# Windowed attention into mixture-of-experts attention on one core: gate, softmax-sum and scale arithmetic moved from VectorE to GpSimd, with a new written-out order

## The chip, the cores and the metric

One core of one Trainium2 chip runs the whole program. A core has TensorE (matmuls, PE in the profile, with PEld for its weight loads), VectorE (DVE), ScalarE (ACT), GpSimd (POOL) and SyncE (SP, which here only issues transfers). The metric is the device time of one execution in microseconds; lower is better.

## The reference

Eight batches of 576 positions. First every head does attention in a sliding window of 64 positions; its eight heads side by side are the input of a layer of four attention experts. A gate picks two of the four experts for each position and weights them.

```python
def _attn_ref(q, k, v):                      # 8 batches, 8 heads, 576 positions, 64 columns
    scores = scale * np.matmul(q, k.transpose(0, 1, 3, 2))
    mask = (rel >= 0) & (rel < 64)
    scores = np.where(mask, scores, -1000000000.0)
    attn = np.exp(scores - np.max(scores, axis=-1, keepdims=True))
    attn = attn / (np.sum(attn, axis=-1, keepdims=True) + 1e-09)
    return np.matmul(attn, v)
...
def _moe_ref(x, w_gate, wq, wk, wv, wo):     # x: 8 x 576 x 512, 4 experts of 64 columns
    logits = x @ w_gate
    topk = np.argpartition(-logits, K, axis=-1)[..., :K]
    w = np.exp(sel)                          # sel: the two chosen logits less the greater
    w /= w.sum(-1, keepdims=True) + 1e-09
    for e in range(E):
        a = np.exp(scores - scores.max(-1, keepdims=True))    # causal
        a /= a.sum(-1, keepdims=True) + 1e-09
        ye = a @ v @ wo[e]
        out += mask[..., None] * w[:, :, kk:kk + 1] * ye
```

## The kernel before

The work is cut into named units, each a Python generator whose steps (from one `yield` to the next) issue a few instructions. A written-out string, `ORDER`, names the unit whose next step is recorded next. Each engine runs its own instructions in just that order, in sequence: an instruction that waits holds back all that stand behind it on its engine. A colon in `ORDER` gives the PSUM banks that the unit takes.

Stage 1 (windowed attention) goes in 72 groups `g` of four tiles. `m` makes scores on TensorE; `q` is `s1_qk`: VectorE adds the mask and finds the row minimum (L320) and, from group 18 on, folds two halves (L328); ScalarE takes exponentials and row sums into `st` (L331); VectorE adds 1e-9 to the sums (L339) and takes the reciprocal (L340); GpSimd multiplies the rows by it (L344). `t` transposes on TensorE and VectorE masks while it copies out (L381); `a` multiplies by the values, and VectorE leaves the rest of a split in two (L405).

Stage 2 goes by batch `b` and pair of experts `pr`. `v` projects values, `g` is `s2_gate`, `k` and `r` project keys and queries, `x` makes scores on TensorE (L609), `y` is `s2_soft`: VectorE masks and finds the minimum (L624), ScalarE takes exponentials (L628). `u` is `s2_w`: for the row sums in `r2` VectorE adds 1e-9 (L658), takes the reciprocal (L659) and multiplies by the gate (L660); then for each of nine rows x ScalarE writes the scaled row as float16 (L671, `hi`), and what float16 leaves (`lo`) comes either from GpSimd in two instructions (L676, L677) or from VectorE in one (L674). `LOW` says which for each row, and from batch 6, pair 1 on (`LATE`) it is VectorE for all. `D` are transposing transfers of `hi` and `lo`, issued by SP; `A` multiplies them by the values on TensorE (L708), and `o` makes the output (L494 to L496 with the weights `wo`).

Stage 1 of later batches runs beside stage 2 of earlier ones, so from about 60 us on all engines work on both. Batch 7 has nothing of stage 1 left beside it.

Of the kernel before, what the change touches and what calls it, by code (L numbers as in the profile page):

```python
# [13 lines left out]
OP = mybir.AluOpType  # L14
AX = mybir.AxisListType
# [5 lines left out]
E = 4  # L21
# [9 lines left out]
LOW = "PPPPPPPPP"  # L31
LATE = (6, 1)


UP = 2.0 ** 15
# [130 lines left out]
def window_attention_moe_attention(ctx: ExitStack, tc: tile.TileContext, qT, kT, vW,  # L166
                                   wg, wq, wk, wv, wo, out):
    nc = tc.nc
# [681 lines left out]
```

## Time and profile before

| | |
|---|---|
| runs | median 484.28 us of 3 (483.62 to 485.56) |
| the profiled execution | 485.02 us, of which the profile's span is 483.3 us |
| mean granted TensorE clock in it | 0.973 of full speed |
| busy in the span | PE 444.5 us, DVE 423.9 us, ACT 357.2 us, POOL 323.9 us |

The span runs from the first to the last instruction that the profiler saw; what lies around it is 1.7 us. An engine's busy time is the time in which it worked on at least one instruction. Neighbours can overlap a little, so the durations of a list's lines add up to somewhat more than the busy time.

### The profile page before, as it was taken

Reading aid. Unit: us, or ns where it says so; the run is one execution under the profiler, and the core shown is the slowest. Engines: PE = TensorE matmul, PEld = TensorE weight load, DVE = VectorE, ACT = ScalarE, POOL = GpSimd, SP = SyncE. Lnnn points to the kernel's source line nnn. Section 1 sums busy time; section 2 is a strip of 40 time slices with the busy share of each in tenths; the row PEclk is TensorE's granted clock in tenths of the full one; section 3 lists DMA queues with packets and bytes.
Section 4 is the critical chain, followed back from the end, with each engine's and each line's share of the span. In section 5 each row is a group of like instructions: output and inputs, shape, how many; then the busy total and the mean of one; then the engine's idle time right before and its main releaser. Section 6 shows DMA issues by size and latency. Waiting matters only on the chain.

```text
span 483.3 us, 17081 instructions
## 1 busy us (share of the span) xinstructions
PE 444.5 (92%) x6192; PEld 391.7 (81%) x6192; DVE 423.9 (88%) x1784; ACT 357.2 (74%) x1304; POOL 323.9 (67%) x682
## 2 busy tenths in 40 slices
PE   7999999989999898988989989989999899999846
PEld 6787898978889798777978979878898779888745
DVE  4797999999999999999998999999999897997730
ACT  5987998787985675786786768767796666768722
POOL 4899698987799758776789575795878676400000
PEclk9999999999999899999999999999999899989959
DMA  8883276968996696766879769386697866468893
GB/s 259 321 306 105 92 158 185 154 173 167 229 213 144 111 224 213 146 148 172 165 181 169 171 160 263 107 154 176 149 203 134 151 138 137 73 110 159 171 174 110
DMA packets 142788, 81.86 MB, mean 169 GB/s; under 512 B 124656, under 2 KB 125680, under 8 KB 142704
## 3 DMA queue, kind: packets, MB, share of 16 engines
q1 hardware_dynamic: 142624, 80.64, 73.1%
q8 instruction: 49, 0.80, 0.7%
q14 instruction: 35, 0.29, 0.2%
q10 hardware_dynamic: 80, 0.13, 0.1%
HBM read 40.90 MB, written 9.44 MB: 104 GB/s over the span
## 4 chain that ended last, share of the span: by engine, by line
DVE 56%; PE 21%; POOL 7%; issue 5%; DMA 5%; ACT 4%; SPq 1%; DVEq 0%; POOLq 0%; ACTq 0%
DVE pt L381 12%; DVE p L624 8%; DVE sm L320 6%; PE ps L708 4%; PE ps L609 4%; DVE p L328 4%; DMA k<-in_kT_dram 3%; DVE xl L405 3%; PE ps L494 3%; PE ps L394 2%; PE ps L496 2%; DVE vr L515 2%; PE ps L495 2%; ACT p L628 2%; PE ps L303 2%
## 5 line engine op out<-in xcount | busy, mean ns | idle before, releaser
L677 POOL TENSOR_TENSOR sp<-p,sp 128x192 f16<-128x192 f32 (+3 forms) x104 | 96.8, 931 | 8.7
L628 ACT ACTIVATE p<-p,r 128x192 f32<-128x192 f32 (+3 forms) x128 | 77.2, 607 | 21.9 <-DVE r L624 15.0
L344 POOL TENSOR_SCALAR p<-p,st 128x64 f32<-128x64 f32 x216 | 64.3, 322 | 32.4 <-DVE st L340 17.8
L331 ACT ACTIVATE p<-p,st 128x64 f32<-128x64 f32 x216 | 72.4, 339 | 17.2 <-DVE p L328 13.3
L671 ACT ACTIVATE sp<-p,r 128x192 f16<-128x192 f32 (+3 forms) x128 | 72.3, 609 | 9.2 <-DMA tu<-sp 6.2
L381 DVE TENSOR_TENSOR pt<-ps,tri 64x512 f32<-64x512 f32 (+1 forms) x120 | 75.5, 633 | 2.8 <-PE ps L394 0.8
L676 POOL TENSOR_SCALAR p<-p,r 128x192 f32<-128x192 f32 (+3 forms) x104 | 63.0, 606 | 17.1 <-ACT sp L671 17.1
L708 PE MATMUL ps<-tu,v 128*64 128x64 f16 (+2 forms) x1760 | 64.4, 233 | 8.7 <-DMA tu<-sp 6.7
L624 DVE CUSTOM_DVE_ANT_0 p<-ps,causal 128x320 f32<-128x320 f32 (+3 forms) x160 | 67.8, 470 | 4.3 <-PE ps L609 2.6
L708 PEld LDWEIGHTS <-v 128*64 128x64 bf16 x1760 | 60.8, 114 | 12.5 <-DMA tu<-sp 6.8
L320 DVE CUSTOM_DVE_ANT_0 sm<-ps,win 128x128 f32<-128x128 f32 x264 | 62.3, 282 | 4.0 <-PE ps L303 2.3
L609 PE MATMUL ps<-kt,qt 64*128 64x256 f32 (+2 forms) x480 | 54.3, 333 | 7.8 <-DVE kt L579 2.4
L609 PEld LDWEIGHTS ps<-kt,qt 64*128 64x128 f32 x480 | 37.8, 185 | 18.6 <-issue 2.6
L303 PE MATMUL ps<-k,q 64*64 64x128 f32 (+1 forms) x1080 | 40.9, 280 | 5.2 <-DMA k<-in_kT_dram 2.8
L303 PEld LDWEIGHTS ps<-k,q 64*64 64x64 f32 x1080 | 31.9, 138 | 12.0 <-issue 4.1
L331 ACT ACTIVATION_READ_ACCUMULATOR p<-p,st 128x1 f32 x216 | 41.2, 191 | 0.0
L494 PE MATMUL ps<-xh,wkhi 128*128 128x320 f32 (+1 forms) x128 | 39.7, 310 | 1.5 <-DVE st L320 0.7
L494 PE MATMUL ps<-xh,wqhi 128*128 128x256 f32 (+1 forms) x128 | 39.3, 307 | 1.5 <-DVE yl L717 0.8
L487 POOL MEMSET sp<- 128x256 f16 (+2 forms) x38 | 10.7, 291 | 44.4 <-DMA tu<-sp 32.7
L394 PE MATMUL ps<-pt,v 128*64 128x64 f32 x1080 | 39.1, 227 | 1.4 <-DVE r L624 0.9
L394 PEld LDWEIGHTS ps<-pt,v 128*64 128x64 f32 x1080 | 34.8, 140 | 6.9 <-DVE r L624 1.3
L496 PE MATMUL ps<-xh,wqlo 128*128 128x256 f32 (+1 forms) x128 | 37.8, 296 | 0.0
(140 smaller groups left out, 1265.8 us busy)
## 6 DMA issues: line engine op xcount, KB each, us to landing
v<-in_vW_dram SPq DMA_DIRECT2D x30, 576.0 KB, 4.9
k<-in_kT_dram SPq DMA_DIRECT2D x29, 320.0 KB, 4.2
q<-in_qT_dram SPq DMA_DIRECT2D x29, 288.0 KB, 3.4
out_dram<-out SPq DMA_DIRECT2D x32, 256.0 KB, 2.7
tu<-sp SPq DMA_TRANSPOSE x96, 3.7
out_dram<-out SPq DMA_DIRECT2D x7, 128.0 KB, 2.5
sp<-in_kT_dram SPq DMA_DIRECT2D x2, 320.0 KB, 6.6
p<-in_qT_dram SPq DMA_DIRECT2D x2, 288.0 KB, 6.4
```

The source lines that it names most:

```text
L303: nc.tensor.matmul(S1[g][i][o:o + 64, c:], lhsT=q_t[r, 64 * b:64 * b + 64], rhs=k_t[r, 64 * b + c:64 * b + 128], start=True, stop=True)
L320: nc.vector.tensor_tensor_reduce(out=to, in0=ps[i][:, c:], in1=win[:, int(b == 0), c:], scale=-0.125, scalar=3.0e38, op0=OP.add, op1=OP.mi ...
L331: nc.scalar.activation(pt[:, i], pt[:, i], AF.Exp, bias=st[:, 0, z + i:z + i + 1], scale=-1.0, accum_out=st[:, 1, z + i:z + i + 1])
L381: nc.vector.tensor_mul(t[64 * w:64 * w + 64, :n, e], ps[r, :n], tri[r, w, None, :].to_broadcast([64, n, 128]))
L394: nc.tensor.matmul(o[64 * h:64 * h + 64, 4 * x + i], lhsT=pairs[p][2][:, h, b], rhs=t[:, i, c:c + 64], start=True, stop=True)
L494: nc.tensor.matmul(ps, lhsT=ah, rhs=bh, start=first, stop=False)
L609: nc.tensor.matmul(ps[e][:, at(i):at(i) + n], lhsT=QT[pr][r, w, q], rhs=KT[b, pr][r, m, key:key + n], start=x == 0, stop=x == 2)
L624: nc.vector.tensor_tensor_reduce(out=dst, in0=src, in1=mask, scale=1.0, scalar=3.0e38, op0=OP.add, op1=OP.min, accum_out=to)
L628: nc.scalar.activation(p, p, AF.Exp, bias=r2[:, 0, x:x + 1], scale=-1.0, accum_out=r2[:, 1, x:x + 1])
L671: nc.scalar.activation(hi, p, AF.Copy, scale=by)
L677: nc.gpsimd.tensor_tensor(lo, p, hi, op=OP.subtract)
L708: nc.tensor.matmul(to, lhsT=V2[b % 2][:, c, a, 2 * pr + h], rhs=rhs, start=n == 0, stop=n == len(work_list) - 1, skip_group_check=True)
```

## The change

Four things change. In `s1_qk` the sum of 1e-9 goes from VectorE to GpSimd, with a step of its own before the reciprocal. In `s2_gate` VectorE keeps the comparisons, the reductions and the reciprocal; the mask product and sum, the subtraction of the maximum, the product with the selection, the 1e-9 and scale, the product with the reciprocal, and the copies into `G2` go to GpSimd, in seven further steps; of two VectorE lines the order is exchanged. In `s2_w` the 1e-9 and the product with the gate go to GpSimd, except from `LATE` on. `LOW` gives row 7 (576 wide) to VectorE, where one instruction takes the place of two on GpSimd. And `ORDER` is another string throughout; two lines of each near its end are shown.

```diff
-LOW = "PPPPPPPPP"
+LOW = "PPPPPPPDP"
...
-    'u701 y710 o54 A601 u700 u700 u700 A611 y710 y710 y710 y710 k711:7 k711 o53 o53 o60:2 u700 u700 D7001 D7001 '
-    'x712:34 x712 k711 k711 x711:57 x711 y711 D7010 D7010 D7011 D7011 u701 o60 u701 A611 A611 A601 A601 u701 u701 '
+    'k711 o53 o53 D7000 D7000 D7010 D7010 D7011 D7011 D7001 D7001 o54 o54 x710:45 x710 x712:31 x712 x711:72 x711 '
+    'u701 y710 y710 y710 y711 u701 u701 u701 u701 u701 y710 y710 y711 y711 o62:6 o60:4 o61:5 o60 o61 D7020 D7020 '
...
-        nc.vector.tensor_scalar_add(st[:, 2, :n], st[:, 1, :n], 1e-9)
+        nc.gpsimd.tensor_scalar(st[:, 2, :n], st[:, 1, :n], 1e-9, 1.0, op0=OP.add, op1=OP.mult)
+        yield
         nc.vector.reciprocal(st[:, 2, :n], st[:, 2, :n])
...
-        nc.vector.tensor_mul(g4[:, 1], g4[:, 1], below[:, None].to_broadcast([128, n, E, E]))
-        nc.vector.tensor_add(g4[:, 0], g4[:, 0], g4[:, 1])
+        yield
+        nc.gpsimd.tensor_tensor(g4[:, 1], g4[:, 1], below[:, None].to_broadcast([128, n, E, E]), op=OP.mult)
+        nc.gpsimd.tensor_tensor(g4[:, 0], g4[:, 0], g4[:, 1], op=OP.add)
+        yield
...
         nc.vector.tensor_reduce(gt[:, 0], g4[:, 0], axis=AX.X, op=OP.add)
+        nc.vector.tensor_reduce(gs[:, 0], lg, axis=AX.X, op=OP.max)
         nc.vector.tensor_scalar(gt[:, 0], gt[:, 0], 1.5, None, op0=OP.is_lt)
-        nc.vector.tensor_reduce(gs[:, 0], lg, axis=AX.X, op=OP.max)
-        nc.vector.tensor_sub(gt[:, 1], lg, gs[:, 0, :, None].to_broadcast([128, n, E]))
+        yield
+        nc.gpsimd.tensor_tensor(gt[:, 1], lg, gs[:, 0, :, None].to_broadcast([128, n, E]), op=OP.subtract)
         yield
         nc.scalar.activation(gt[:, 1], gt[:, 1], AF.Exp)
         yield
-        nc.vector.tensor_mul(gt[:, 1], gt[:, 1], gt[:, 0])
+        nc.gpsimd.tensor_tensor(gt[:, 1], gt[:, 1], gt[:, 0], op=OP.mult)
+        yield
         nc.vector.tensor_reduce(gs[:, 1], gt[:, 1], axis=AX.X, op=OP.add)
-        nc.vector.tensor_scalar(gs[:, 1], gs[:, 1], 1e-9, 1.0 / UP, op0=OP.add, op1=OP.mult)
+        yield
+        nc.gpsimd.tensor_scalar(gs[:, 1], gs[:, 1], 1e-9, 1.0 / UP, op0=OP.add, op1=OP.mult)
+        yield
         nc.vector.reciprocal(gs[:, 2], gs[:, 1])
-        nc.vector.tensor_mul(gt[:, 2], gt[:, 1], gs[:, 2, :, None].to_broadcast([128, n, E]))
+        yield
+        nc.gpsimd.tensor_tensor(gt[:, 2], gt[:, 1], gs[:, 2, :, None].to_broadcast([128, n, E]), op=OP.mult)
...
-            nc.vector.tensor_copy(dst[0:64], src[64:128])
-            nc.vector.tensor_copy(dst[64:128, 0:3], src[0:64, 1:4])
+            nc.gpsimd.tensor_copy(dst[0:64], src[64:128])
+            nc.gpsimd.tensor_copy(dst[64:128, 0:3], src[0:64, 1:4])
...
-        nc.vector.tensor_scalar_add(r2[:, 2, x], r2[:, 1, x], 1e-9)
+        engine = nc.vector if (b, pr) >= LATE else nc.gpsimd
+        engine.tensor_scalar(r2[:, 2, x], r2[:, 1, x], 1e-9, 1.0, op0=OP.add, op1=OP.mult)
+        yield
         nc.vector.reciprocal(r2[:, 2, x], r2[:, 2, x])
-        nc.vector.tensor_mul(r2[:, 3, x], r2[:, 2, x], G2[b % 2][:, pr, x])
+        yield
+        engine.tensor_tensor(r2[:, 3, x], r2[:, 2, x], G2[b % 2][:, pr, x], op=OP.mult)
         yield
```

What stands on VectorE at the gate of batch 3 before the change, with row scales of batches 2 and 3 (`r2`) beside it (`gt` and `gs` are the gate's tiles, `g2` its result, `yl` and `xl` rests of splits that TensorE waits for):

```order
L405 TENSOR_TENSOR xl4_4012<-ps_67,xh4_4011 128x512
L542 TENSOR_TENSOR gt_3_0_3957<-gt_3_0_3957 128x16
L543 TENSOR_REDUCE gs_3_0_3958<-gt_3_0_3957 128x4
L544 TENSOR_SCALAR gs_3_0_3958<-gs_3_0_3958 128x4
L545 RECIPROCAL gs_3_0_3958<-gs_3_0_3958 128x4
L546 TENSOR_TENSOR gt_3_0_3957<-gt_3_0_3957,gs_3_0_3958 128x16
L551 COPY g2_1_90<-gt_3_0_3957 64x4x2x2
L552 COPY g2_1_90<-gt_3_0_3957 64x3x2x2
L554 COPY g2_1_90<-gt_3_0_3957 64x2 x2
L717 TENSOR_TENSOR yl1_86<-ps_67,yh1_84 128x320
L658 TENSOR_SCALAR r2_3_0_3872<-r2_3_0_3872 128x7
L659 RECIPROCAL r2_3_0_3872<-r2_3_0_3872 128x7
```

Nine small instructions of the gate stand in a row here, ahead of `yl1`. After the change VectorE has, at the same gate (lines 390 and up are those of the new file; `qt` and `kt` are rests that the scores on TensorE wait for):

```order
L677 RECIPROCAL r2_2_1_3363<-r2_2_1_3363 128x2
L390 TENSOR_TENSOR pt1_44_4107<-ps_67,tri_78 64x2x128
L609 TENSOR_TENSOR qt0_81<-ps_67,qt0_81 128x256
L595 TENSOR_TENSOR kt_3_0_3837<-ps_67,kt_3_0_3837 128x256
L390 TENSOR_TENSOR pt1_43_4112<-ps_67,tri_78 64x4x128
L560 RECIPROCAL gs_3_0_3950<-gs_3_0_3950 128x4
L390 TENSOR_TENSOR pt1_44_4107<-ps_67,tri_78 64x2x128
L390 TENSOR_TENSOR pt1_43_4112<-ps_67,tri_78 64x4x128
```

Only the reciprocals are left, and each stands among large instructions that wait for other things. On GpSimd, at the same place, the order before has only large work of rows (`p2`, `px`) and of stage 1 (`p1`):

```order
L344 TENSOR_SCALAR p1_45_4004<-p1_45_4004,st1_44_3933 128x64 x4
L487 MEMSET sp1_72 128x4x64
L676 TENSOR_SCALAR p2_1_69<-p2_1_69,r2_2_1_3454 128x576
L677 TENSOR_TENSOR sp1_72<-p2_1_69,sp1_72 128x576
L676 TENSOR_SCALAR p2_1_69<-p2_1_69,r2_2_1_3454 128x576
L677 TENSOR_TENSOR sp1_72<-p2_1_69,sp1_72 128x576
L676 TENSOR_SCALAR px_70<-px_70,r2_3_0_3872 128x64
```

After the change the same stretch of GpSimd reads:

```order
L675 TENSOR_SCALAR r2_2_1_3363<-r2_2_1_3363 128x2
L679 TENSOR_TENSOR r2_2_1_3363<-r2_2_1_3363,g2_0_89 128x2
L558 TENSOR_SCALAR gs_3_0_3950<-gs_3_0_3950 128x4
L353 TENSOR_SCALAR p1_45_3826<-p1_45_3826,st1_44_3813 128x64 x4
L695 TENSOR_SCALAR p2_1_69<-p2_1_69,r2_2_1_3363 128x448
L696 TENSOR_TENSOR sp1_72<-p2_1_69,sp1_72 128x448
L562 TENSOR_TENSOR gt_3_0_3949<-gt_3_0_3949,gs_3_0_3950 128x16
L567 COPY g2_1_90<-gt_3_0_3949 64x4x2x2
L568 COPY g2_1_90<-gt_3_0_3949 64x3x2x2
L570 COPY g2_1_90<-gt_3_0_3949 64x2 x2
L675 TENSOR_SCALAR r2_3_0_4042<-r2_3_0_4042 128x7
```

The small instructions now stand here, between the rows' work, and those at L679, L558 and L562 wait for VectorE. The third place is the start of GpSimd's work on stage 1 (`sm` are the first groups' rows, `st` their sums). Before:

```order
L344 TENSOR_SCALAR sm1_0_151<-sm1_0_151,st1_0_150 128x128 x4
L344 TENSOR_SCALAR sm1_1_225<-sm1_1_225,st1_1_224 128x128 x4
L344 TENSOR_SCALAR sm1_2_237<-sm1_2_237,st1_2_236 128x128 x4
L344 TENSOR_SCALAR sm1_3_249<-sm1_3_249,st1_3_248 128x128 x4
L479 MEMSET v2_1_91 64x768
```

And after:

```order
L488 MEMSET v2_0_92 64x768
L347 TENSOR_SCALAR st1_0_179<-st1_0_179 128x4
L353 TENSOR_SCALAR sm1_0_180<-sm1_0_180,st1_0_179 128x128 x4
L347 TENSOR_SCALAR st1_1_185<-st1_1_185 128x4
L353 TENSOR_SCALAR sm1_1_186<-sm1_1_186,st1_1_185 128x128 x4
L347 TENSOR_SCALAR st1_2_205<-st1_2_205 128x4
L347 TENSOR_SCALAR st1_3_209<-st1_3_209 128x4
L353 TENSOR_SCALAR sm1_2_206<-sm1_2_206,st1_2_205 128x128 x4
```

Each group's rows now have an addition ahead of them on GpSimd, with VectorE's reciprocal between the two.

## Rows read from the trace of the kernel before

**Rows 1.** The page's first part: busy time, share of the span and instructions by engine.
```profile
PE 444.5 (92%) x6192; PEld 391.7 (81%) x6192; DVE 423.9 (88%) x1784; ACT 357.2 (74%) x1304; POOL 323.9 (67%) x682
```

**Rows 2.** Windows: length, each engine's busy time (instructions), clock, DMA share, GB/s.
```profile
60.00:400.00 340.00, 319.07 (x4548) 283.26 (x4548) 324.89 (x1321) 258.61 (x970) 263.66 (x535) 0.99 0.78 170
...
20.00:40.00 20.00, 19.53 (x325) 17.13 (x319) 16.48 (x79) 16.45 (x63) 18.52 (x46) 1.00 0.63 221
40.00:60.00 20.00, 19.75 (x286) 17.05 (x287) 18.00 (x102) 18.43 (x71) 15.36 (x40) 1.00 0.35 110
...
400.00:420.00 20.00, 20.00 (x211) 19.03 (x207) 16.31 (x63) 14.58 (x45) 12.28 (x19) 1.00 0.54 94
420.00:440.00 20.00, 18.89 (x259) 16.47 (x259) 17.68 (x75) 13.00 (x39) 0.94 (x3) 0.91 0.65 124
```

**Rows 3.** PE's waits, 60 to 400 us: us in total, times, longest.
```profile
PE ps L494 <- DVE vr L515: 2.5, 3, 1.4
...
PE ps L494 <- ACT yh L715: 1.1, 1, 1.1
...
PE ps L494 <- DVE pt L381: 0.2, 1, 0.2
```

**Rows 4.** The page's fourth part: the chain that ended last, by engine.
```profile
DVE 56%; PE 21%; POOL 7%; issue 5%; DMA 5%; ACT 4%; SPq 1%; DVEq 0%; POOLq 0%; ACTq 0%
```

**Rows 5.** VectorE's groups, 60 to 400 us: count, busy us, mean ns, idle before.
```profile
L660 DVE TENSOR_TENSOR r<-r,g 128x7 f32<-128x7 f32 (+1 forms) x24 | 8.5, 355 | 0.8
L658 DVE TENSOR_SCALAR r<-r 128x7 f32<-128x7 f32 (+1 forms) x24 | 7.3, 303 | 0.2
L339 DVE TENSOR_SCALAR st<-st 128x8 f32<-128x8 f32 x27 | 6.4, 236 | 0.3 <-ACT p L331 0.2
L531 DVE TENSOR_TENSOR g<-g,below 128x64 f32<-128x64 f32 (+1 forms) x9 | 5.7, 635 | 0.3
...
L552 DVE COPY g<-gt 64x12 f32<-64x12 f32 x6 | 1.0, 162 | 0.1
```

**Rows 6.** Timeline, VectorE and GpSimd near 221 us, and VectorE late: start, us.
```profile
221.44 1.29 POOL L677 TENSOR_TENSOR sp<-p,sp 128x576 f16<-128x576 f32 x1
...
221.70 1.05 DVE L660 TENSOR_TENSOR r<-r,g 128x7 f32<-128x7 f32 x1
...
452.36 0.17 DVE L660 TENSOR_TENSOR r<-r,g 128x7 f32<-128x7 f32 x1
```

**Rows 7.** GpSimd's groups by form, 60 to 400 us; last, one of the whole run.
```profile
L344 POOL TENSOR_SCALAR p<-p,st 128x64 f32<-128x64 f32 x216 | 64.3, 322 | 32.4 <-DVE st L340 17.8 <-ACT p L331 4.7 <-PE ps L609 3.0
L677 POOL TENSOR_TENSOR sp<-p,sp 128x576 f16<-128x576 f32 x24 | 31.0, 1291 | 2.0
...
L676 POOL TENSOR_SCALAR p<-p,r 128x576 f32<-128x576 f32 x24 | 19.1, 797 | 11.9 <-ACT sp L671 11.9
...
L677 POOL TENSOR_TENSOR sp<-px,sp 128x64 f16<-128x64 f32 x13 | 4.3, 329 | 1.1
...
L474 POOL MEMSET below<- 128x16 f32 x1 | 0.1, 118 | 0.0
```

**Rows 8.** Groups by form, whole run: one operation on both engines, and VectorE's row rest.
```profile
L519 POOL TENSOR_TENSOR v<-vr,v 128x256 bf16<-128x256 f32 x28 | 19.8, 706 | 2.3
...
L519 DVE TENSOR_TENSOR v<-vr,v 128x256 bf16<-128x256 f32 x4 | 2.8, 688 | 0.1
...
L674 DVE SCALAR_TENSOR_TENSOR sp<-p,r,sp 128x576 f16<-128x576 f32 x6 | 4.7, 812 | 3.5 <-DMA tu<-sp 3.5
```

**Rows 9.** Windows: the first 8 to 52 us, columns as in the second group.
```profile
8.00:52.00 44.00, 41.15 (x629) 34.84 (x629) 35.22 (x197) 37.86 (x160) 38.66 (x94) 0.96 0.67 240
```

**Rows 10.** Timeline of PE near the end: start, us, count, idle before.
```profile
465.19 2.61 PE L708 MATMUL ps<-tu,v 128*64 128x256 f16 x50 [6.68 <-DMA tu<-sp]
```

**Rows 11.** Waits of SP's queue, whole run: us in total, times, longest.
```profile
SPq L685 <- POOL p L676: 30.3, 20, 4.6
SPq L685 <- POOL sp L677: 27.5, 17, 3.0
```

More of the change, by code (lines that the diff above doesn't have):

```diff
@@ L550, in s2_gate @@
             dst = G2[b % 2][:, :, 1:9].rearrange("r p (j s) -> r j p s", s=2)
-            nc.vector.tensor_copy(dst[0:64], src[64:128])
-            nc.vector.tensor_copy(dst[64:128, 0:3], src[0:64, 1:4])
+            nc.gpsimd.tensor_copy(dst[0:64], src[64:128])
+            nc.gpsimd.tensor_copy(dst[64:128, 0:3], src[0:64, 1:4])
             for s in range(2):
-                nc.vector.tensor_copy(G2[b % 2][64 * s:64 * s + 64, :, 0], src[0:64, 0, :, s])
+                nc.gpsimd.tensor_copy(G2[b % 2][64 * s:64 * s + 64, :, 0], src[0:64, 0, :, s])
         else:
             for h in range(2):
-                nc.vector.tensor_copy(G2[h][64:128, :, 7:9], src[64 * h:64 * h + 64, 0])
+                nc.gpsimd.tensor_copy(G2[h][64:128, :, 7:9], src[64 * h:64 * h + 64, 0])
     def proj(b, name, pr, half):
```

251 rows, old and new, of the table ORDER are left out of this document.

## The prediction

> **What bounds the kernel now.** I read the page's busy times first [rows 1]: PE is busy for 92% of the span and DVE for 88%, so neither alone explains the time. The windows show how they share it [rows 2]. Between 60 and 400 us, where stage 1 and stage 2 run side by side, DVE works for 324.9 of 340 us (95.6%) and PE for 319.1. PE's waits in that stretch [rows 3] say why PE is idle for the other 20.9 us: of 21 lines all but one (ACT, 1.1 us) name a DVE instruction that TensorE's next matmul needs or whose PSUM bank it takes over. The chain that ended last goes through DVE for 56% of its length and through PE for 21% [rows 4]. So in the middle DVE is the engine that is out of time and PE follows it. POOL is busy for 263.7 of the 340 us there (78%).
>
> The two ends are different. From 8 to 52 us POOL has the work: 38.7 of 44 us, against 35.2 on DVE [rows 9]. Near the end PE stands still for 6.68 us, waiting for transposing transfers of `hi` and `lo` [rows 10]; POOL has almost nothing left then.
>
> **What the change takes from VectorE.** Thirteen lines of DVE go to POOL. Between 60 and 400 us they are, from L660 (24 times, 8.5 us) down to L552 (6 times, 1.0 us), 159 instructions and 51.9 us [rows 5]. That is 0.33 us for each of these tiny instructions, and the timeline shows what is in it: L660 took 1.05 us at 221.70 and ended within 0.02 us of POOL's 1.29 us instruction that had begun at 221.44; late, with POOL idle, the same instruction took 0.17 us [rows 6]. Some of what leaves DVE is thus time spent standing behind POOL.
>
> What comes to DVE is row 7's rest, 13 instructions, 12 of them in this stretch. Beside an idle POOL one takes 0.81 us [rows 8]. Beside a busy one it reads two tiles as L660 does, so it may stand behind a POOL instruction of up to 1.29 us [rows 7]: bounds 10 and 25 us for the twelve. I take 1.0 us each, 12 us, since L660's mean excess over its undisturbed 0.17 us is 0.19 us. Net, DVE goes from 324.9 to 285 us (bounds 283 and 298).
>
> How much of PE's idle time does that return? I take it from stretches of this run where DVE has less work than PE. In 20 to 40, 40 to 60, 400 to 420 and 420 to 440 us DVE has 0.84, 0.91, 0.82 and 0.94 of PE's busy time, and PE is idle for 0.47, 0.25, 0.00 and 1.11 us: 1.8 of 80 us, 2.3% [rows 2]. The middle would go from 1.02 to 285/319 = 0.89, so I give it that 2.3%: 7.8 us idle in place of 20.9, **a gain of 13 us**. Bounds: 19 (PE idle 2 us, nothing but a last remainder) and 0.
>
> **What the change gives to GpSimd.** There is no POOL row for additions or copies this small. From above: no instruction of 64 columns takes more than 0.33 us; from below: a memset of 16 columns takes 0.12 us [rows 7]. Between them I draw lines through two widths: L344 at 64 and L676 at 576 columns (0.322 and 0.797 us) give 0.26 us plus 0.9 ns a column, L677 (0.329 and 1.291 us) gives 0.21 us plus 1.9 ns. At 2 to 64 columns that is 0.21 to 0.33; I take 0.25 us on average. 159 of them cost 40 us. Row 7 takes away 12 times 0.797 and 12 times 1.291 us, 25 us. POOL goes from 263.7 to 279 us, 82% of the stretch. From below it is 257 us; from above, with the 0.08 us that stands idle ahead of each L677 (2.0 us in 24) added to each new one, 304 us, 89%. POOL was 93% busy between 20 and 40 us (18.5 of 20) and PE lost 0.47 us, so 82% alone costs nothing. I put **0** here; the hand-offs are a rival below.
>
> The Trainium skill says otherwise: GPSIMD Engine Reference, section 4.1 (Engine selection), puts elementwise work of two inputs on VectorE, GpSimd being about twice as slow. One operation stands on both engines here, L519, and took 706 ns on POOL and 688 ns on DVE [rows 8]; that row doesn't show the factor. By this page of the Trainium skill the 51.9 us would become 104 us on POOL, which would need 239 + 104 = 343 us for the 340.
>
> **The new waits.** A softmax sum now goes ACT, POOL, DVE, POOL instead of ACT, DVE, POOL; a row's scale goes POOL, DVE, POOL; a gate crosses between DVE and POOL seven times. Behind DVE's waiting reciprocals stand the rests `kt` and `qt` that the scores wait for; behind POOL's L558 and L562 stand the rows that SP's transfers wait for. The order places other work between, and PE waits only if a whole engine runs late.
>
> **The start.** By 52 us POOL also has 18 additions for the first groups and 11 instructions of batch 0's gate, 29 at 0.25 us: 7.3 us. It is idle for 5.3 of the 44 us [rows 9], so between 2 and 7 us of this come on top if PE has nothing else. I take **3 us lost**, near the lower bound, because the order also moves a clearing of `v2` into POOL's first idle time.
>
> **The end.** From `LATE` on nothing moves. After the scores `x711` the old order leaves PE `x713`, three outputs and the two products `A70`, the new one four outputs and the same; the transfers for `A710` hang on the same DVE and ACT work. **0**, bounds 2 gained and 4 lost.
>
> **Sum.** The profiled execution took 485.0 us. 485.0 - 13 + 3 = 475.0 us; the median lies 0.7 us below that execution, so **474.3 us**. This case's own range is 467 to 481: below, 19 gained in the middle and 2 lost at the start; above, 7 lost at the start and, in the middle, 3 of the 11 us that the slice at 0.94 (5.5% idle, 18.9 us) would add to 7.8.
>
> **Rivals.**
>
> *GpSimd becomes the bound (slower).* POOL takes each of its instructions in turn, and each new one may wait for DVE. DVE was the bound at 95.6% of the stretch; POOL reaches that share of 340 us when a new instruction costs (325 - 239)/159 = 0.54 us with its wait, and from there all of the gain is gone. At 0.55 us the middle takes 341 us, and the start's 29 cost 16 us against 5.3 idle, 11 us lost: 485.0 + 1 + 11 - 0.7 = 496 us. For it: every new instruction depends on another engine's. Against it: the prices above, and POOL's 78% now. The factor of two in the Trainium skill (GPSIMD Engine Reference, section 4.1) leads to the same place, 343 us for POOL. Chance 0.16.
>
> *The waits move, the time stays.* PE stops waiting for DVE and waits for what POOL feeds. SP's transfers already wait 27.5 and 30.3 us for POOL's row instructions [rows 11], and a net 15 us of POOL work in front of them makes these later. If PE's idle time stays near 20 us, the gain of 13 becomes 0 and the start's 3 us are made up by the order: 484 us. Against it: L708, which uses these transfers, waited for one only once, at the end [rows 10]. Chance 0.12.
>
> *TensorE alone is the bound.* In 400 to 420 us PE lost nothing at a ratio of 0.82 [rows 2]. If the middle loses 2 us in all, and POOL's start hides behind other work: 485.0 - 19 - 0.7 = 465 us. Chance 0.11.
>
> *The forecast.* Chance 0.61.
>
> **How the numbers follow.** A measurement of this kernel tells a change from none at about 0.5%, 2.4 us. Faster holds the forecast and TensorE's case, 0.72; the case without gain is 0.12; slower is 0.16. The range runs from 465, TensorE's case, less one, to 488: this holds the forecast's own 467 to 481 and the case without gain; what it leaves out is most of the GpSimd rival and a little below 464, less than 2 in 10.
>
> **What would show it.** Right: DVE busy near 385 us in all and under 90% of the middle; PE's waits on DVE there 8 us or less; POOL between 330 and 355 us, with L347 and L675 at 0.23 to 0.27 us; the thirteen new L693 near 1.0 us. Wrong in the middle: PE's idle time there still above 15 us, or named by POOL. Wrong at the start: PE idle more than 5 us between 20 and 60 us. What would make the prediction wrong altogether is a POOL instruction of few columns that takes 0.5 us or more, copies between partition halves above all, for which nothing in this trace has a price.

## The result, and the profile after

The changed kernel took 467.68 us (median of 4 runs, 466.91 to 468.84) beside 483.95 us for the kernel before on the same chip: a ratio of 0.9661 (95% interval 0.9629 to 0.9692). The profiled execution took 467.63 us, 17.4 us less than that of the kernel before.

The page's busy times, to lay beside [rows 1], and the chain by engine, beside [rows 4]:

```profile
PE 438.8 (94%) x6192; PEld 388.9 (83%) x6192; DVE 376.6 (81%) x1588; ACT 357.2 (77%) x1304; POOL 347.3 (75%) x865
...
PE 21%; DVE 9%; ACT 8%; POOL 7%; DMA 4%; issue 3%; SPq 0%; DVEq 0%; POOLq 0%; ACTq 0%
```

DVE works 47.3 us less than before, POOL 23.4 us more. The chain's shares add up to 52% here, since it could be followed back no further than 218 us; before they add up to 99%. So 9% is not to be held against the 56% of [rows 4] as it stands: of the part that was followed, DVE has 9 of 52, an estimated 17%. Windows of the changed kernel, columns as in [rows 2]:

```profile
0.00:60.00 60.00, 54.10 (x719) 46.09 (x720) 39.38 (x221) 45.90 (x189) 49.37 (x145) 1.00 0.57 196
60.00:385.00 325.00, 313.40 (x4584) 279.94 (x4584) 288.58 (x1186) 260.74 (x976) 279.76 (x676) 1.00 0.79 179
385.00:465.90 80.90, 71.30 (x896) 62.88 (x894) 48.59 (x182) 50.57 (x140) 18.20 (x46) 0.94 0.75 146
```

And the two stretches of the kernel before that stand around its 60 to 400 us in [rows 2]:

```profile
0.00:60.00 60.00, 55.08 (x808) 46.82 (x809) 45.85 (x267) 49.24 (x198) 46.06 (x124) 0.97 0.63 216
400.00:483.30 83.30, 70.32 (x846) 61.60 (x842) 53.18 (x198) 49.38 (x137) 14.15 (x25) 0.91 0.67 133
```

Subtract PE's busy time from each length. At the start PE was idle for 4.9 us and now is for 5.9; in the middle 20.9 and now 11.6; at the end 13.0 and now 9.6. Together this is 11.7 us less idle time. (How it divides is rough, since the stretches of the two kernels hold nearly, not quite, the same work.) The other 5.7 us are in PE's busy time, 444.5 against 438.8 for the same 6192 matmuls. In the middle DVE is now at 88.8%, and POOL at 86%.

PE's waits of the changed kernel, 60 to 385 us (beside [rows 3]):

```profile
PE ps L503 <- DVE pt L390: 1.9, 2, 1.1
PE ps L625 <- DVE vr L524: 1.2, 1, 1.2
PE ps L503 <- DVE vr L524: 1.2, 2, 0.8
...
PE ps L376 <- POOL p L353: 0.7, 3, 0.2
```

Twelve of the 17 lines of this view name DVE, 8.6 us in all by their printed values; POOL has 0.7 us. In the kernel before, the 20 lines that named DVE added up to 19.6 us.

The prices on GpSimd, by form, whole run (beside [rows 7]; L347 is the softmax sum, L675 and L679 the scale's, L541 and L570 the gate's):

```profile
L353 POOL TENSOR_SCALAR p<-p,st 128x64 f32<-128x64 f32 x216 | 67.6, 336 | 5.4 <-DVE st L349 4.5
...
L528 POOL TENSOR_TENSOR v<-vr,v 128x256 bf16<-128x256 f32 x28 | 21.2, 757 | 2.3
...
L347 POOL TENSOR_SCALAR st<-st 128x8 f32<-128x8 f32 x27 | 5.4, 201 | 5.9 <-ACT p L339 3.9
...
L347 POOL TENSOR_SCALAR st<-st 128x4 f32<-128x4 f32 x18 | 4.3, 240 | 4.1 <-ACT sm L339 2.7
...
L570 POOL COPY g<-gt 64x2 f32<-64x2 f32 x16 | 3.4, 214 | 0.7
L675 POOL TENSOR_SCALAR r<-r 128x7 f32<-128x7 f32 x13 | 3.3, 253 | 3.2 <-ACT px L644 2.3
...
L679 POOL TENSOR_TENSOR r<-r,g 128x7 f32<-128x7 f32 x13 | 2.7, 210 | 1.5 <-DVE r L677 1.3
...
L541 POOL TENSOR_TENSOR g<-g,below 128x64 f32<-128x64 f32 x8 | 2.6, 320 | 0.3 <-DVE g L539 0.3
L675 POOL TENSOR_SCALAR r<-r 128x2 f32<-128x2 f32 x13 | 2.5, 193 | 1.5 <-ACT p L644 0.5
```

All 209 moved instructions add up to 46 us there, 0.22 us each. And two groups of VectorE, by form, whole run (beside [rows 8]):

```profile
L693 DVE SCALAR_TENSOR_TENSOR sp<-p,r,sp 128x576 f16<-128x576 f32 x19 | 16.2, 864 | 4.4 <-DMA tu<-sp 2.9 <-ACT sp L690 1.4
...
L528 DVE TENSOR_TENSOR v<-vr,v 128x256 bf16<-128x256 f32 x4 | 1.7, 426 | 0.1
```

### The profile page after: what moved, and what is told of

The parts are those of the page before. It is cut to its first block, busy times and chain, and to the rows that moved or that the text cites. A ratio compares the mean times of both kernels' runs of the same rounds, so it can differ in the third digit from the quotient of the medians.

```text
span 465.9 us, 17032 instructions
## 1 busy us (share of the span) xinstructions
PE 438.8 (94%) x6192; PEld 388.9 (83%) x6192; DVE 376.6 (81%) x1588; ACT 357.2 (77%) x1304; POOL 347.3 (75%) x865
## 4 chain that ended last, share of the span: by engine, by line
PE 21%; DVE 9%; ACT 8%; POOL 7%; DMA 4%; issue 3%; SPq 0%; DVEq 0%; POOLq 0%; ACTq 0%
PE ps L727 4%; PE ps L503 4%; DMA tu<-sp 4%; PE ps L504 3%; PE ps L505 3%; PE ps L625 3%; ACT sp L690 3%; ACT p L339 2%; PE ps L403 2%; ACT p L644 2%; POOL sp L696 2%; POOL p L353 1%; DVE sm L328 1%; DVE pt L390 1%; DVE p L336 1%
## 5 line engine op out<-in xcount | busy, mean ns | idle before, releaser
L644 ACT ACTIVATE p<-p,r 128x576 f32<-128x576 f32 (+3 forms) x128 | 77.3, 606 | 23.7 <-DVE r L640 12.1
L696 POOL TENSOR_TENSOR sp<-p,sp 128x320 f16<-128x320 f32 (+3 forms) x91 | 80.7, 886 | 7.6
L690 ACT ACTIVATE sp<-p,r 128x192 f16<-128x192 f32 (+3 forms) x128 | 73.1, 607 | 11.7 <-DMA tu<-sp 7.0
L353 POOL TENSOR_SCALAR p<-p,st 128x64 f32<-128x64 f32 x216 | 67.6, 336 | 5.4 <-DVE st L349 4.5
L640 DVE CUSTOM_DVE_ANT_0 p<-ps,causal 128x320 f32<-128x320 f32 (+3 forms) x160 | 68.2, 471 | 3.7 <-POOL sp L696 2.2
L727 PE MATMUL ps<-tu,v 128*64 128x64 f16 (+2 forms) x1760 | 62.1, 229 | 5.3 <-DMA tu<-sp 4.8
L727 PEld LDWEIGHTS <-v 128*64 128x64 bf16 x1760 | 59.0, 112 | 8.9 <-issue 6.7
L695 POOL TENSOR_SCALAR p<-p,r 128x320 f32<-128x320 f32 (+3 forms) x91 | 53.6, 589 | 5.1 <-ACT sp L690 4.2
L625 PE MATMUL ps<-kt,qt 64*128 64x320 f32 (+2 forms) x480 | 50.5, 328 | 3.1 <-DVE vr L524 1.2
L625 PEld LDWEIGHTS ps<-kt,qt 64*128 64x128 f32 x480 | 36.1, 185 | 12.6 <-DVE vr L524 1.6
L503 PE MATMUL ps<-wvhi,xh 128*128 128x260 f32 x128 | 37.3, 292 | 2.7 <-DVE pt L390 1.9
L503 PE MATMUL ps<-xh,wkhi 128*128 128x256 f32 (+1 forms) x128 | 39.5, 309 | 0.3 <-DVE vr L524 0.2
```

Source lines behind the costliest of these rows:

```text
L353: nc.gpsimd.tensor_scalar(p, p, st[:, 2, i:i + 1], 1.0, op0=OP.mult, op1=OP.mult)
L503: nc.tensor.matmul(ps, lhsT=ah, rhs=bh, start=first, stop=False)
L625: nc.tensor.matmul(ps[e][:, at(i):at(i) + n], lhsT=QT[pr][r, w, q], rhs=KT[b, pr][r, m, key:key + n], start=x == 0, stop=x == 2)
L640: nc.vector.tensor_tensor_reduce(out=dst, in0=src, in1=mask, scale=1.0, scalar=3.0e38, op0=OP.add, op1=OP.min, accum_out=to)
L644: nc.scalar.activation(p, p, AF.Exp, bias=r2[:, 0, x:x + 1], scale=-1.0, accum_out=r2[:, 1, x:x + 1])
L690: nc.scalar.activation(hi, p, AF.Copy, scale=by)
```

## The experiments

Each run was timed beside the kernel before on the same chip. "Moved" are the small operations of sums, gate and scales; D is VectorE, P GpSimd. Busy times, span and idle time (span less busy time) are those of one profiled execution. The kernel before had medians of 483.8 to 485.1 us beside these runs, so medians of different runs that lie a microsecond or two apart are compared by their ratios.

| kernel | median us | ratio to before (95%) | DVE busy | POOL busy | span | POOL idle |
|---|---|---|---|---|---|---|
| before | 483.95 | | 423.9 | 323.9 | 483.3 | 159.4 |
| changed | 467.68 | 0.966 (0.963 to 0.969) | 376.6 | 347.3 | 465.9 | 118.6 |
| new order only | 492.66 | 1.017 (1.011 to 1.023) | 407.2 | 325.8 | 489.0 | 163.2 |
| old order, moves only | 559.43 | 1.154 (1.147 to 1.162) | 372.2 | 348.0 | 554.7 | 206.7 |
| row 7 back on P | 488.06 | 1.008 (1.005 to 1.011) | 369.4 | 369.2 | 487.4 | 118.2 |
| moved ones back on D | 487.67 | 1.005 (1.003 to 1.007) | 412.0 | 304.7 | 486.1 | 181.4 |
| moved ones doubled on P | 507.25 | 1.046 (1.042 to 1.050) | 373.7 | 387.3 | 505.3 | 118.0 |
| D padded | 473.14 | 0.976 (0.973 to 0.978) | 391.7 | 347.5 | 471.4 | 123.9 |
| reciprocals in the same step | 506.14 | 1.042 (1.035 to 1.049) | 374.6 | 346.0 | 503.0 | 157.0 |
| gate back on D | 477.40 | 0.983 (0.979 to 0.986) | 395.7 | 324.4 | 475.5 | 151.1 |
| row 8 for row 7 | 470.30 | 0.970 (0.965 to 0.975) | 374.7 | 348.0 | 467.2 | 119.2 |
| row 8 on D too | 466.25 | 0.960 (0.956 to 0.964) | 381.4 | 325.9 | 461.7 | 135.8 |
| first sums on D | 467.27 | 0.964 (0.961 to 0.967) | 378.7 | 344.3 | 463.3 | 119.0 |
| row 8 and first sums on D | 464.74 | 0.957 (0.954 to 0.960) | 383.8 | 321.4 | 463.3 | 141.9 |

**The order without the moves.** In the changed kernel the moved lines go back to VectorE and row 7 to GpSimd:

```diff
-LOW = "PPPPPPPDP"
+LOW = "PPPPPPPPP"
...
-        nc.gpsimd.tensor_scalar(st[:, 2, :n], ...
+        nc.vector.tensor_scalar(st[:, 2, :n], ...
-        engine = nc.vector if (b, pr) >= LATE else nc.gpsimd
+        engine = nc.vector
```
(and the gate's ten lines likewise)

> The changed kernel's order and steps, with every moved operation and row 7 where they were before (the small operations on VectorE, row 7's rest on GpSimd). Theory (VectorE's relief is the gain): VectorE works for some 420 us again, about 95% of the middle, and TensorE waits about 20 us for it: 482 to 492 us, no better than the kernel before. Rival (the new order is the gain, the engines do not matter): TensorE's idle time in the middle stays near 12 us and the time at 467 to 473 us.

492.66 us, just above the 482 to 492 that the theory gave: the new order and its steps without the moves gain nothing, they lose 1.7%. The theory's mechanism was not met as well as its time. VectorE worked for 407.2 us in all, not 420, and for 293.4 of the 325 us from 60 to 385 us, 90% and not 95%; TensorE still had 26.9 us idle there, more than in the kernel before. So VectorE's load alone does not explain this time. That an order written for the other loads fits these badly is likely, but no run shows it.

**The moves without the order.** The kernel before with its old steps and string:

```diff
-LOW = "PPPPPPPPP"
+LOW = "PPPPPPPDP"
-        nc.vector.tensor_scalar_add(st[:, 2, :n], st[:, 1, :n], 1e-9)
+        nc.gpsimd.tensor_scalar(st[:, 2, :n], st[:, 1, :n], 1e-9, 1.0, op0=OP.add, op1=OP.mult)
         nc.vector.reciprocal(st[:, 2, :n], st[:, 2, :n])
```
(scales and gate likewise, with no new steps)

> The kernel before with its old order and steps, and only the moves: sums, gate and scales on GpSimd, row 7's rest on VectorE. Theory: VectorE falls to about 380 us and TensorE's waits for it fall with it, 468 to 476 us, the hand-offs costing some us since the old order puts no work between them. Rival (the new order is the gain): 482 us or more, TensorE still waiting 20 us, now for work behind the hand-offs.

559.43 us. VectorE is as free as in the changed kernel (372.2 us), and yet the kernel is 76 us slower than before. The waits of VectorE in this run (us in total, times, longest; here L660 is the scale's reciprocal and L340 the sum's):

```profile
DVE r L660 <- POOL r L659: 32.7, 17, 8.7
DVE st L340 <- POOL st L339: 31.8, 24, 6.3
DVE gt L535 <- POOL g L532: 22.4, 12, 4.5
```

What stands behind these waits on DVE is late, and TensorE, with a busy time of 468.9 us, is idle for 85.8 of its 554.7. My theory had the hand-offs at "some us"; the loss is more than four times the gain.

**The steps alone.** In the changed kernel the reciprocals of sums and scales are recorded right with their additions:

```diff
         nc.gpsimd.tensor_scalar(st[:, 2, :n], ...
-        yield
         nc.vector.reciprocal(st[:, 2, :n], st[:, 2, :n])
         yield
+        yield
```
(scales likewise)

> The changed kernel with the reciprocals of softmax sums and scales recorded in the same step as the GpSimd addition that they wait for, so that no other VectorE work stands between; prices and engines unchanged. If the finer steps are what made the hand-offs cheap (theory; the old order with the moves and without the steps took 559 us): 485 us or more, VectorE's waits for the additions up from 14 us to 40 or more. If that loss came from the old order as a whole (rival): 467 to 475 us.

506.14 us, 38 us more than the changed kernel, with the same instructions on the same engines and the same string. VectorE's waits in it:

```profile
DVE st L348 <- POOL st L347: 38.5, 28, 3.5
DVE r L676 <- POOL r L675: 25.6, 18, 4.2
```

In the changed kernel the first of these was:

```profile
DVE st L349 <- POOL st L347: 11.1, 12, 1.9
```

So it is the separate step, with other work recorded between, that makes the move pay.

**Row 7 back on GpSimd.**

```diff
-LOW = "PPPPPPPDP"
+LOW = "PPPPPPPPP"
```

> The changed kernel with row 7 back on GpSimd. VectorE loses some 11 us, GpSimd gains some 27 and comes to about 95% of the stretch from 60 to 385 us. If GpSimd has room (theory): within 2 us of the changed kernel. If GpSimd is near being the bound (rival): 4 to 10 us longer, with TensorE or ScalarE waiting for it. If VectorE at 89% still sets the time (second rival): 2 to 6 us shorter.

488.06 us: 21.9 us more on POOL cost 20.4 us, more than any of the three expectations. The middle of this run:

```profile
60.00:385.00 325.00, 304.08 (x4398) 270.26 (x4397) 267.67 (x1137) 249.25 (x929) 284.55 (x664) 0.98 0.76 172
```

And its two largest waits of VectorE (L640 is stage 2's row minimum):

```profile
DVE st L349 <- POOL st L347: 18.6, 17, 5.4
DVE p L640 <- POOL sp L696: 15.6, 12, 2.4
```

VectorE is less busy than in the changed kernel (267.7 against 288.6 us) and still late, since it waits for GpSimd; POOL, at 87.6% of the stretch, is hardly busier than in the changed kernel (86%).

**The moved ones back, row 7 left on VectorE.** The first diff of this section without the change of `LOW`.

> The changed kernel with all small operations (sums, gate, scales) back on VectorE and row 7's rest left on VectorE. With the changed kernel and the runs with row 7 back and with all back it makes a table of two by two under one order. If both moves are needed (theory): VectorE works for some 415 us, TensorE waits for it some 20 us, 480 to 490 us. If taking row 7 off GpSimd is the whole gain (rival): 466 to 471 us.

487.67 us, as the theory had it. This fills a table of two by two: both moves 467.7, row 7 alone 487.7, the small ones alone 488.1, neither 492.7 us. Under this order each alone is worth 5 us and both together 25. The 25 are not the change's gain: beside the kernel before, with its own order, that is 16.3 us.

**GpSimd's price doubled.** 185 of the 209 moved instructions are issued twice (POOL has 1050 instructions in this run and 865 in the changed kernel; the expectation says 191), such as:

```diff
         nc.gpsimd.tensor_scalar(st[:, 2, :n], st[:, 1, :n], 1e-9, 1.0, op0=OP.add, op1=OP.mult)
+        nc.gpsimd.tensor_scalar(st[:, 2, :n], st[:, 1, :n], 1e-9, 1.0, op0=OP.add, op1=OP.mult)
```

> The changed kernel with most of the moved instructions (191 of 209) issued twice on GpSimd, so that each has the price of two, about 0.44 us, below the 0.54 us from which the prediction's rival has GpSimd as the bound. GpSimd gains some 42 us, 33 of them between 60 and 385 us, and comes to about 96% there. If it has room: within 2 us. If it is near being the bound: 5 to 12 us longer, as VectorE's 96% cost TensorE 21 us idle in the kernel before against 12 now.

507.25 us, far outside both expectations: 40.0 us more on POOL cost 39.6 us. The chain by engine of this run:

```profile
POOL 47%; DVE 16%; PE 15%; ACT 11%; issue 7%; DMA 3%; SPq 1%; POOLq 0%; DVEq 0%; ACTq 0%
```

Read with the table: POOL's idle time is 118.6, 118.2 and 118.0 us in the changed kernel, with row 7 back, and doubled. Not one microsecond of the added work went into it. VectorE's waits say where it went. Its largest wait for POOL, 11.1 us in the changed kernel and 18.6 with row 7 back, is here:

```profile
DVE st L350 <- POOL st L348: 24.7, 23, 2.8
```

All lines of VectorE's waits that name POOL add up to 5.7 us in the kernel before, 30.2 in the changed one, 53.5 with row 7 back and 71.3 doubled: 23 and 41 us more than in the changed kernel, close to the 20.4 and 39.6 that the two runs cost. TensorE's waits for VectorE, 9.9 us in the changed kernel, are 19.2 and 27.4 us in these two runs, for POOL 2.2, 3.9 and 6.3. So work that makes POOL late reaches TensorE mostly through VectorE, which stands still at the hand-offs; that is how work added to an engine with a quarter of its time idle can be paid in full.

**VectorE padded.** A maximum over a constant tile, which nothing reads, behind each of 89 reciprocals:

```diff
         nc.vector.reciprocal(r2[:, 2, x], r2[:, 2, x])
+        nc.vector.tensor_reduce(pad, ident, axis=AX.X, op=OP.max)
```

> The changed kernel with 89 more instructions on VectorE that nothing uses (a maximum over a constant tile of 128x128, right behind each reciprocal of sums, gate and scales; an estimated 0.2 us each, 18 us in all). It is the counterpart of the run with row 7 back, which put 22 us more on GpSimd and cost 20 us. If GpSimd is the engine that sets the changed kernel's time (theory now), VectorE still has room: 467 to 474 us. If any work added to any engine under this fixed order is paid in full (rival): 483 to 488 us.

473.14 us. The three padded places, VectorE's groups:

```profile
L350 DVE TENSOR_REDUCE pad<-ident 128x1 f32<-128x128 f32 x45 | 11.2, 248 | 0.0
...
L681 DVE TENSOR_REDUCE pad<-ident 128x1 f32<-128x128 f32 x32 | 8.1, 253 | 0.0
...
L563 DVE TENSOR_REDUCE pad<-ident 128x1 f32<-128x128 f32 x12 | 3.1, 257 | 0.0
```

22.4 us of instructions raised DVE's busy time by 15.1 us and the time by 5.5, 0.36 us for each microsecond of busy time; row 7 on GpSimd cost 20.4 us for 21.9, 0.93. That rules out the rival that any work on any engine is paid in full. The padding stands behind the reciprocals, not ahead of them as the doubled additions do, so it shows VectorE's room at this place only.

**Row 8 in place of row 7.** `LOW = "PPPPPPPPD"`.

> The changed kernel with row 7's rest back on GpSimd and row 8's, of the same width, on VectorE instead: the loads of both engines are those of the changed kernel, and only the place differs. If it is GpSimd's load that made the run with row 7 back 20 us longer (theory): 466 to 472 us. If the place of row 7's rest in the queues did (rival): 478 us or more.

470.30 us, not told apart from the changed kernel (the intervals overlap). So it was GpSimd's load that made the run with row 7 back longer, and not that row's place.

**The gate back on VectorE.** The gate's ten lines as in the first diff, sums and scales left on GpSimd.

> The changed kernel with the gate's small operations and copies back on VectorE, the finest of the new steps left as they are. VectorE gains an estimated 20 us, GpSimd loses an estimated 25. By the 0.36 us that a microsecond more on VectorE cost (run with padding): 473 to 477 us. If the gate's seven crossings cost what they save (rival): 465 to 469 us.

477.40 us, just above the 473 to 477 of the first expectation: DVE +19.1 us, POOL -22.9 us, time +9.7. Taking the gate's part of the move back costs more than half of the whole gain, in spite of the seven crossings that go with it.

**Less on GpSimd.** Row 8 on VectorE too (`LOW = "PPPPPPPDD"`), and, apart from it, the first groups' sums:

```diff
-        nc.gpsimd.tensor_scalar(st[:, 2, :n], ...
+        (nc.vector if g < FIRST else nc.gpsimd).tensor_scalar(st[:, 2, :n], ...
```

> The changed kernel with row 8's rest on VectorE too: some 22 to 25 us off GpSimd, 11 us on to VectorE. If GpSimd sets the changed kernel's time (theory now): 455 to 463 us. If VectorE at 89% still does, or the order was fitted to these loads alone (rival): 467 to 476 us.

> The changed kernel with the 18 softmax-sum additions of the first groups back on VectorE, where the prediction lost 3 us at the start. GpSimd is busy for 18.7 of 20 us between 20 and 40 us. If the additions cost something there: 464 to 467 us. If the start loses nothing to them (rival): 467 to 469 us.

466.25 and 467.27 us, neither told apart from the changed kernel. The theory that GpSimd sets the changed kernel's time (455 to 463 us with row 8 moved) failed here: 21.4 us less on POOL, for 4.8 more on DVE, brought 1.4 us between the medians. So GpSimd's work costs when it is added and gives little when it is taken away. In the profiled execution 17.2 of the 21.4 us went into POOL's own idle time, 118.6 to 135.8 us.

**Both together.**

> The changed kernel with row 8's rest and the first groups' sums on VectorE, both of which alone were not slower than the changed kernel. If GpSimd's load still takes something at the start and VectorE has room for both: 462 to 466 us. If the order leaves no more to be had: 466 to 469 us.

464.74 us (463.38 to 465.19), as the first expectation had it, ratio 0.9567 (0.9539 to 0.9595). Its interval lies below the changed kernel's: about 1%, 3 to 4.5 us, faster than that, and the fastest kernel here.

## Why the prediction held, and where its steps did not

The time lay 6.6 us below the predicted 474.3, at the lowest edge of the forecast's own range of 467 to 481. The mechanism held: VectorE was relieved, and TensorE's idle time in the middle fell with its waits for VectorE. That the time still fell within the range is in part luck: the sum had 10 us gained and the execution gained 17.4, and of the missing 7.4 us 5.7 are in a term that the sum did not have. In number 467.7 is nearer to the rival with TensorE alone as the bound (465) than to 474.3, but that rival had 2 us idle in the middle, and 11.6 were measured. By the terms of the sum:

- **The middle, 13 us gained.** Measured 9.3 us (20.9 to 11.6 idle). DVE came to 0.92 of PE's busy time (288.6/313.4), not 0.89, and the idle share to 3.6%, not 2.3%; that lies between the prediction's slices at 0.91 (1.3% idle) and 0.94 (5.5%), so the dependence on the ratio was about right. PE's waits there name DVE with 8.6 us where I had set 8 or less. Row 7's rests were cheaper than the 1.0 us that I took: the twelve between 60 and 400 us have a mean of 0.892 us.
- **The start, 3 us lost.** Measured 1.0 us up to 60 us. The first sums on VectorE gave a difference too small to measure.
- **The end, 0.** Measured 3.4 us gained; I had 2 as the bound. "From `LATE` on nothing moves" was not right either: batch 7's gate, which moves too, began at 427 us in the kernel before, behind the first late rest at 417 us. The long wait for transposing transfers [rows 10] is 4.22 us now, 6.68 before, as the timeline of PE shows:

```profile
448.68 1.17 PE L727 MATMUL ps<-tu,v 128*64 128x256 f16 x20 [4.22 <-DMA tu<-sp]
```

- **Missing: PE's busy time, 5.7 us.** The sum counted idle time alone. Windows of the kernel before, 2 us each, around two of TensorE's waits (columns as in [rows 2]):

```profile
158.00:160.00 2.00, 0.56 (x3) 0.18 (x1) 1.96 (x9) 0.53 (x1) 0.00 (x0) 1.00 1.02 289
160.00:162.00 2.00, 1.97 (x31) 1.71 (x35) 1.93 (x9) 1.60 (x7) 1.38 (x5) 0.63 0.62 119
162.00:164.00 2.00, 2.00 (x39) 1.67 (x33) 1.97 (x12) 1.53 (x5) 1.92 (x7) 0.52 0.00 0
380.00:382.00 2.00, 0.83 (x5) 0.46 (x5) 1.93 (x6) 0.02 (x1) 1.04 (x1) 1.00 0.70 110
382.00:384.00 2.00, 2.00 (x7) 1.51 (x8) 1.94 (x4) 1.79 (x9) 0.00 (x0) 0.60 0.97 229
384.00:386.00 2.00, 2.00 (x18) 1.23 (x18) 1.31 (x4) 0.70 (x3) 1.14 (x4) 0.55 0.12 41
```

PE worked for 0.56 and 0.83 of 2 us there, DVE for nearly all of it, and in the next 4 us the granted clock was 0.52 to 0.63, most of the time the lower level (1.2 GHz). PE counts as busy in these windows while its clock is low. The page's clock by slices, before and then after:

```profile
PEclk9999999999999899999999999999999899989959
```

```profile
PEclk9999999999999999999999999999999999999979
```

The dips in the middle are gone with the waits. Mean clock times span gives an estimate: 13.0 us of full clock were withheld before (2.7% of 483.3) and 4.7 after (1.0% of 465.9). The 8.3 us between them are enough for the 5.7. Windows of 5 us put 1.7, 3.4 and 7.8 us of it at the start, in the middle and at the end of the kernel before, and all 4.6 at the end of the changed one: the middle has less than half of the difference. And the clock is not all of it: at the same mean clock of 0.987 PE was busy for 443.8 us in the run with the new order only and for 437.7 with row 8 and the first sums on D. No run separates the clock from other causes, so this cause stays open.

- **GpSimd, 0.** The size was about right and its reason was not. Prices (0.22 us where I had 0.25; L347 at 0.20 to 0.24 and L675 at 0.19 to 0.25 where I had 0.23 to 0.27) and POOL's busy time (347, within 330 to 355) were close, TensorE's waits in the middle name POOL with 0.7 us, and 21.4 us less on POOL brought 1.4. But "82% alone costs nothing" took POOL's idle share for room, and the rival's deciding price, 0.54 us an instruction, came from that. By the runs, POOL work added to the changed kernel is paid in full: the gain of 16.3 us would be gone after about as many microseconds, at an estimated (46 + 16.5)/209 = 0.30 us. Doubled, at about 0.41 us (46 + 40 us over 209), the kernel is already 23 us slower than before. By these runs the forecast lay much nearer the slower rival than its chance of 0.16 says.
- **The hand-offs, 0.** "The order places other work between" was the right reason: VectorE's waits for POOL rose from 5.7 to 30.2 us, and TensorE's for VectorE fell all the same. What hung on it was larger than anything in the sum: 38 us when sums and scales lose their separate step, 76 us slower than before with the old order. The rival of waits that move did not come: TensorE waited 4.8 us for transposing transfers over the run, 6.7 before.

The prediction said that the L519 rows did not show GpSimd's factor of two. That was a misreading: in the row of 688 ns one of four had stood beside a POOL instruction of 1.29 us and taken 1.47 us, the other three 0.43 each, as the timeline of the kernel before shows:

```profile
414.74 1.29 POOL L677 TENSOR_TENSOR sp<-p,sp 128x576 f16<-128x576 f32 x1
...
414.84 1.47 DVE L519 TENSOR_TENSOR v<-vr,v 128x256 bf16<-128x256 f32 x1
419.88 0.43 DVE L519 TENSOR_TENSOR v<-vr,v 128x256 bf16<-128x256 f32 x1
```

The same operation, now L528, takes 757 ns on POOL and 426 ns on DVE, 1.8 times. At this width the trace agrees with the Trainium skill (GPSIMD Engine Reference, section 4.1, Engine selection), whose factor of about two is for operations of two inputs. The prediction's 104 us doubled the additions of a constant and the copies with them; the same row of the Trainium skill has work of one input at roughly line rate. Only the lines with two inputs, 26.8 of the 51.9 us, would double: an estimated 79 us and not 104, and 318 us of POOL's 340, not 343. Neither figure decided, because the moved instructions are so small that 46 us is what all 209 cost on POOL, where before 159 of them had cost 51.9 us on DVE [rows 5].

POOL's busy share, the smallest of the five in the page of the profile, is not where one would look for the bound. The Trainium skill (Perfetto Trace Analysis, Identifying the Most-Contended Engine) says to take the engine with the highest occupancy as the bottleneck, and not to judge TensorE by its matmuls' busy share but, among others, by that of its weight loads. Before the change the trace agrees: VectorE has 88% and the weight loads have 81% [rows 1], and relieving VectorE under a new order gave 16 us. For the changed kernel the share does not tell what more work costs: at 75% busy GpSimd is the engine on which it is paid in full, though 21.4 us less of it brought 1.4.

What stays open: every variant but the one with the old order keeps the order of the changed kernel, so how much of these costs a newly searched order would take back was not tried. Nor was moving the sums alone or the scales alone.

## What to carry to other kernels

Moving small work off a full engine paid here only where something else was queued between the instruction that waits and the one it waits for, so count the new hand-offs as closely as the instructions. An engine's idle time under a fixed order need not be room: double the work that is to go there, and see whether the time follows. Where TensorE's idle time is priced, look at its granted clock behind each wait too.

## What the runs showed of the hardware

- GpSimd's price of a small instruction hardly depends on its size: in the changed kernel 201 ns for 128x8, 240 for 128x4, 214 for a copy of 64x2; at 128x64 it is 320.
- The same 1784 VectorE instructions took 423.9 us in the old order and 407.2 in the new one (run with the order only). Part of it is the gate's product with the mask, and the scale's product with the gate. VectorE's groups, whole run, in the kernel before:

```profile
L660 DVE TENSOR_TENSOR r<-r,g 128x7 f32<-128x7 f32 (+1 forms) x32 | 9.9, 309 | 1.1
...
L531 DVE TENSOR_TENSOR g<-g,below 128x64 f32<-128x64 f32 (+1 forms) x12 | 6.5, 540 | 0.4
```

and in the run with the new order only:

```profile
L679 DVE TENSOR_TENSOR r<-r,g 128x7 f32<-128x7 f32 (+1 forms) x32 | 6.5, 204 | 0.6
...
L541 DVE TENSOR_TENSOR g<-g,below 128x64 f32<-128x64 f32 (+1 forms) x12 | 3.5, 291 | 0.1
```

I read this as the order deciding how often they stand beside a GpSimd instruction, as in the two cases above ([rows 6] and the one at 414.84 us); the runs do not count these cases.

- PE's busy time for the same 6192 matmuls went from 436.2 us (row 8 on VectorE too, granted clock 0.993) to 468.9 us (old order with the moves, 0.929).
